# Retention in half chunks: 64x64 products in place of 64x128 and 128x64 ones, state summed in PSUM, GEMM products from chunk 5 on

## The chip, the core and the metric

The kernel runs on one core of a Trainium2 chip. The metric is the device time of one execution, in microseconds. The kernel before took 580.88 us (median of 3 runs, 578.93 to 582.52).

## What is computed

Retention over 2 batches x 8 heads x 768 positions with head dimension 64, then two MLPs over the 1536 resulting rows, all in float32:

```python
for t in range(S):
    state = gamma[None, :, None, None] * state + np.einsum('bhd,bhe->bhde', k[:, :, t], v[:, :, t])
    y[:, :, t] = scale * np.einsum('bhd,bhde->bhe', q[:, :, t], state)
...
h = x @ w_in                                  # 1536x512 @ 512x2048
sp = np.where(h > 20.0, h, np.log1p(np.exp(np.minimum(h, 20.0))))
x = (h * np.tanh(sp)) @ w_out                 # 2048x512
h = x @ w2_in
out = (h * np.cos(h)) @ w2_out
```

The weights arrive as float64 bits; the kernel splits them, and the activations, into a high and a low part, so that each product of a GEMM is three fp32r products (high x high, high x low, low x high).

## The kernel before

**Retention.** The 1536 positions are 12 chunks of 128: chunks 0 to 5 are the first sequence, 6 to 11 the second. q, k, v of a chunk are one load of 1 MiB (`att_load`, in two halves for chunks 0 to 4: first q and k, then v and k in the other layout). For each chunk TensorE does four groups of 8 fp32 products; an fp32 product stands in the trace as two matmul records, so a group is "x16":

- scores (`att_scores`, L330): k times q of the chunk, 64 rows and 128 columns of the array, 128 columns moved; VectorE multiplies the result with a mask of decays (`att_mask`, L335)
- inter (`att_inter`, L376): the state of the chunks before times the scaled q, 64x64 of the array, 128 columns moved; not in chunks 0 and 6
- update (`att_update`, L346): k times the scaled v, 128x64 of the array, 64 columns moved; VectorE adds it to the decayed state (`att_state`, L353, L355), and GpSimd decays the state for the next chunk (`att_scaled`)
- out (`att_out`, L387): v times the masked scores, 128x64 of the array, 128 columns moved; then ScalarE and VectorE split the result into the high and the low part of x (L401, L404)

GpSimd makes the scaled q (`att_qd`) and the scaled v (`att_vd`; ScalarE makes that of chunks 1 to 4).

**GEMMs.** Four chunks make one block of 512 rows of x. A GEMM product of the first kind (`gemm1`, L427) takes 128x128 weights and 512 moved columns. A weight item is named by (which, group, half): ("i", 0, 0) is the first half of the first group of w_in, in two pieces n = 0, 1 of 512 KiB. Pieces of the first w_in are loaded "crossed" (three transfers of 64 or 128 partitions with runs of 1 KiB, L210 and L213), except the `EARLY` one, which is loaded whole (L207) and crossed by the split instead (`w_rows`). The first 96 GEMM products are dealt between the chunks, from chunk 3 on (`deal`); the second GEMM (`gemm2`, L450) starts when retention is over and its PSUM is free (`close`).

**Order.** A planner (`Plan`) takes TensorE's order as the code writes it, and sets the order of the other queues, SP's loads among them, by a list schedule over costs in the code.

Of the kernel before, what the change touches and what calls it, by code (L numbers as in the profile page):

```python
# [20 lines left out]
C = 128  # L21
# [11 lines left out]
VD_ACT = (1, 5)  # L33
EARLY = (("i", 0, 0), 0)
QD_DVE = ()
# [8 lines left out]
TERMS = ((0, 0), (0, 1), (1, 0))  # L44


def shape_constants():
    gamma = (1.0 - 2.0 ** (-5.0 - np.arange(H, dtype=np.float32))).astype(np.float64)
    i = np.arange(C, dtype=np.float64)
    half = np.arange(128) // D  # L50

    doublings = 2.0 ** np.arange(7)
    heads = [2 * a + e for e in range(2) for a in range(NPAIR)]
    first = gamma[heads][None, :] ** -i[:, None] / math.sqrt(D)
    grow = np.broadcast_to(gamma[heads][None, None, :] ** doublings[None, :, None], (128, 7, 8))
    upper = (i[None, :] >= i[:, None]).astype(np.float64)
    of = np.stack([gamma[2 * a + half] for a in range(NPAIR)], axis=1)
    first_q = of / math.sqrt(D)
    grow_q = of[:, None, :] ** doublings[None, :, None]
    decv = gamma[None, :] ** (C - 1.0 - i[:, None])  # L60
    parts = [decv, of**C, first, grow, first_q, grow_q, upper]
    packed = np.concatenate([p.reshape(128, -1) for p in parts], axis=1)
    return np.ascontiguousarray(packed.astype(np.float32))


class Plan:
# [47 lines left out]
    def order(self):  # L114
# [20 lines left out]
        free = {o["engine"]: 1.4 if o["engine"] == "SP" else 0.0 for o in ops}  # L135
        pool = shared = (0.0, 0.0)
        self.start, self.end, order = {}, {}, []
        while ready:
# [32 lines left out]
def retention_two_mlps(ctx: ExitStack, tc: tile.TileContext, qkv, w1i, w1o, w2i, w2o, consts, out):  # L171
# [25 lines left out]
    def w_load(it, ns):  # L197
# [74 lines left out]
    def w_low_part(it, ns, single):  # L272
        eng = nc.vector if single else nc.gpsimd
        for to, of in w_rows(it, ns):
# [12 lines left out]
    scaled = {}  # L287
    update = {}
# [20 lines left out]
    def att_vd(g, part):  # L309
# [3 lines left out]
        if not VD_ACT[0] <= g < VD_ACT[1]:  # L313
            nc.gpsimd.tensor_mul(out=vd[g], in0=v, in1=decv.unsqueeze(2).to_broadcast([128, H, D]))
            return
        for h in range(H // 2 * part, H // 2 * (part + 1)):
            nc.scalar.activation(out=vd[g][:, h, :], in_=v[:, h, :], func=AF.Copy, scale=decv[:, h : h + 1])

    def att_qd(g, eng):
        qd[g] = att_p.tile([128, NPAIR, C], F32, tag="qd", name="qd")  # L320
        eng.tensor_mul(out=qd[g], in0=qk_of(g)[:, :, 0, :], in1=decq)


    def att_scores(g):
        qk = qk_of(g)
        ss = ps_p.tile([128, 2, NPAIR, C], F32, tag="s", name="ps_s")
        for a in range(NPAIR):
            for e in range(2):
                h = slice(D * e, D * e + D)
                nc.tensor.matmul(ss[:, e, a, :], qk[h, a, 1, :], qk[h, a, 0, :], start=True, stop=True)  # L330
        pm[g] = ss

    def att_mask(g):
        p = att_p.tile([128, 2, NPAIR, C], F32, tag="p", name="p")
        nc.vector.tensor_mul(  # L335
            out=p.rearrange("p e a b -> p (e a b)"), in0=pm[g].rearrange("p e a b -> p (e a b)"), in1=mask
        )
        pm[g] = p

    def att_update(g):  # L340
        kn = att[g][:, 1536:2048].rearrange("p (a b) -> p a b", a=NPAIR)
        ps = ps_p.tile([128, NPAIR, D], F32, tag="u", name="ps_u", bufs=2)
        for a in range(NPAIR):
            for e in range(2):
                h = slice(D * e, D * e + D)
                nc.tensor.matmul(ps[h, a, :], kn[:, a, h], vd[g][:, 2 * a + e, :], start=True, stop=True)  # L346
        update[g] = ps


    def att_state(g):  # L350
        state[g] = att_p.tile([128, NPAIR, D], F32, tag="st", name="st")
        if g % NCH == 0:
            nc.vector.tensor_copy(out=state[g], in_=update[g])  # L353
        else:
            nc.vector.tensor_add(out=state[g], in0=update[g], in1=scaled[g])  # L355

    def att_scaled(g):
        scaled[g + 1] = att_p.tile([128, NPAIR, D], F32, tag="sc", name="scaled")
        nc.gpsimd.tensor_mul(out=scaled[g + 1], in0=state[g], in1=carry)

    def y_tag(g):
        return "h0" if g in (0, 2) else "y"

    def att_y(g):
        if g not in y_t:
            pool, tag = (h_p, "h0") if y_tag(g) == "h0" else (ps_p, "y")
            ps = pool.tile([128, 2, BLK], F32, tag=tag, name="ps_y")
            y_t[g] = ps[:, :, 0 : BLK // 2].rearrange("p r (s c) -> p r s c", c=C)
        return y_t[g]

    def att_inter(g):
        ps = att_y(g)
        for a in range(NPAIR):
            for e in range(2):
                h = slice(D * e, D * e + D)
                nc.tensor.matmul(  # L376
                    ps[y_rows(a, e), a % 2, a // 2, :], state[g - 1][h, a, :], qd[g][h, a, :],
                    start=(a < 2), stop=False, skip_group_check=True,
                )

    def att_out(g):
        c = g % NCH
        v = att[g][:, 1024:1536].rearrange("p (h d) -> p h d", h=H)
        ps = att_y(g)
        for a in range(NPAIR):
            for e in range(2):
                nc.tensor.matmul(  # L387
                    ps[y_rows(a, e), a % 2, a // 2, :], v[:, 2 * a + e, :], pm[g][:, e, a, :],
                    start=(c == 0), stop=True, skip_group_check=True,
                )  # L390

# [141 lines left out]
    def weight(it, between=lambda: None):  # L533
        raw, mag, w = ("raw", it), ("mag", it), ("w", it)
        first, single = it[:2] == ("i", 0), it[:2] in (("i", 0), ("o", 0), ("i", 1))
        slow = [1.5 if it[0] == "i" and it[1] < NG and (it, n) != EARLY else 1.0 for n in range(2)]
        if single:
            loads = [op("SP", 1.25 * slow[0], w_load, it, (0,), new=(raw, 2))]
            between()
            loads.append(op("SP", 1.25 * slow[1], w_load, it, (1,), uses=[raw]))  # L540
        else:
            loads = [op("SP", 2.5 * slow[0], w_load, it, (0, 1), new=(raw, 2))]
        for load, ns in zip(loads, [slice(0, 1), slice(1, 2)] if single else [slice(0, 2)]):
# [11 lines left out]
            early, sign = (it, ns.start) == EARLY, last  # L555
# [5 lines left out]
            def high_op(needs):  # L561
                return op("ACT", 1.08 if early else 1.08 * c, w_high_part, it, ns, needs=needs, uses=[mag, w])
# [6 lines left out]
            for n in range(ns.start, ns.stop):  # L569
                at["wh", it, n] = high  # L570
            on_dve = single
            last = op(
                *(("DVE", 1.3 if early else 0.72) if on_dve else ("POOL", 2.45 * c)), w_low_part, it, ns, on_dve,
                needs=[high, low], uses=[w, raw if single else mag],
            )
# [17 lines left out]
    def chunk_pre(g):  # L593
        c = g % NCH
        key = chunk(g)
        on_act = VD_ACT[0] <= g < VD_ACT[1]
        if c + 1 < NCH:
            at["vd", g] = [
                op(
                    *(("ACT", 0.98) if on_act else ("POOL", 1.15)), att_vd, g, part, needs=at["v", g] + at["dec"],  # L600
                    new=None if part else (("vd", g), 2), uses=[key, ("vd", g)],
                )
                for part in range(2 if on_act else 1)
            ]
        if c > 0:
            name, cost, eng = ("DVE", 0.72, nc.vector) if g in QD_DVE else ("POOL", 1.3, nc.gpsimd)
            at["qd", g] = op(
                name, cost, att_qd, g, eng, needs=at["qk", g] + at["decq"], new=(("qd", g), 2), uses=[key]
            )

    def chunk_scores(g):
        s = ("s", g)
        at["s", g] = op("PE", 1.1, att_scores, g, needs=at["qk", g], new=(s, 1, "s"), uses=[chunk(g)])
        at["p", g] = op("DVE", 1.25, att_mask, g, needs=[at["s", g]] + at["mask"], new=(("p", g), 2), uses=[s])

    def chunk_update(g):
        c = g % NCH
        if c + 1 == NCH:
            return
        u = ("u", g)  # L620
        at["u", g] = op(
            "PE", 0.62, att_update, g, needs=at["vd", g] + at["k", g], new=(u, 2), uses=[chunk(g), ("vd", g)]
        )
# [297 lines left out]
```

## Time and profile before

| | |
|---|---|
| median of 3 runs | 580.88 us (578.93 to 582.52) |
| profiled execution, its own time | 582.62 us |
| its span, first to last instruction | 580.8 us |
| end of the last TensorE group | 577.6 us from the span's start |
| TensorE busy | 570.0 us (98%) |
| DMA busy share, 20 to 40 us | 1.0 (326 and 317 GB/s) |

All times in the views are microseconds from the start of the span. "Idle before" an instruction is the time in which its engine had nothing to run, with the engine or transfer whose end released it. PEclk is the granted clock of TensorE as a share of 2.4 GHz.

### The profile page before, as it was taken

To read this page: it belongs to the slowest core of one execution; us is meant where nothing else is said; L and a number is where in the kernel's file an instruction comes from. 1 tells how busy PE (TensorE), PEld (TensorE's weight loads), DVE (VectorE), ACT (ScalarE), POOL (GpSimd) and SP (SyncE) were. 2 spreads that over 40 slices of the span, in tenths; PEclk is the share of its full clock that TensorE was granted. 3 is DMA by queue.
4 is the path that set the end of the run, shared out by engine and by line. 5 is a ranking of instruction groups with operands and counts; after the bars stand their busy time and mean duration, and the time that the engine had idled before them with its cause. 6 is when DMAs were issued, how large, how long until landed. Compare 5 with 4: busy or idle time off the path is not lost.

```text
span 580.8 us, 7248 instructions
## 1 busy us (share of the span) xinstructions
PE 570.0 (98%) x3054; PEld 469.2 (81%) x3054; DVE 385.1 (66%) x410; ACT 225.5 (39%) x255; POOL 96.2 (17%) x63
## 2 busy tenths in 40 slices
PE   8789999999999999999999999999999999999997
PEld 6567888888888888888888888888888888888886
DVE  5678889744185524655377995988588994865462
ACT  3633343334023123123235564575254353354240
POOL 5355100212011111102011102023010403000000
PEclk9989999999999999999999999999999999999999
DMA  8996044353004220312003031224003020000103
GB/s 294 310 290 247 30 145 143 104 159 103 0 9 137 74 72 1 144 73 72 1 19 127 1 106 40 73 72 146 0 1 122 24 73 1 0 1 0 73 36 109
DMA packets 19952, 49.87 MB, mean 86 GB/s; under 512 B 2000, under 2 KB 10064, under 8 KB 19024
## 3 DMA queue, kind: packets, MB, share of 16 engines
q1 hardware_dynamic: 19920, 49.41, 25.2%
q8 instruction: 24, 0.39, 0.3%
q14 instruction: 8, 0.07, 0.0%
HBM read 46.26 MB, written 3.15 MB: 85 GB/s over the span
## 4 chain that ended last, share of the span: by engine, by line
PE 93%; DMA 5%; SPq 1%; ACT 0%; DVE 0%; issue 0%; DVEq 0%; ACTq 0%
PE ps_o L450 45%; PE ps_h L427 45%; DMA qkv<-qkv_dram 4%; DMA raw<-w1i_dram 2%; PE ps_s L330 1%; PE ps_y L387 1%; PE ps_y L376 1%; SPq L304 0%; PE ps_u L346 0%; ACT L454 0%; DVE p L335 0%; ACT mag L218 0%; ACT x L401 0%; DVE acc L515 0%; SPq L740 0%
## 5 line engine op out<-in xcount | busy, mean ns | idle before, releaser
L427 PE MATMUL ps_h<-x,wi 128*128 128x512 f32 x1152 | 268.2, 391 | 0.9 <-DVE wi L275 0.4
L427 PEld LDWEIGHTS ps_h<-x,wi 128*128 128x128 f32 x1152 | 215.7, 188 | 47.6 <-DVE wi L275 1.2
L450 PE MATMUL ps_o<-wo,g 128*128 128x512 f32 (+1 forms) x588 | 132.5, 385 | 0.0
L450 PE MATMUL ps_o<-g,wo 128*128 128x512 f32 x576 | 132.3, 389 | 0.0
L450 PEld LDWEIGHTS ps_o<-wo,g 128*128 128x128 f32 x588 | 108.9, 188 | 22.0
L450 PEld LDWEIGHTS ps_o<-g,wo 128*128 128x128 f32 x576 | 108.1, 188 | 22.4
L492 DVE TENSOR_TENSOR g<-mish,g 128x1024 fp32r<-128x1024 f32 x24 | 33.7, 1404 | 56.6 <-ACT g L488 55.6
L275 POOL TENSOR_TENSOR wo<-mag,wo 128x1024 fp32r<-128x1024 f32 x14 | 35.4, 2526 | 202.4 <-ACT wo L261 202.4
L508 DVE TENSOR_TENSOR acc<-ps_o,acc 128x1024 f32<-128x1024 f32 x35 | 42.7, 1221 | 34.6 <-PE ps_o L450 34.4
L275 POOL TENSOR_TENSOR wi<-mag,wi 128x1024 fp32r<-128x1024 f32 x12 | 30.2, 2520 | 194.1 <-ACT wi L261 194.1
L458 ACT ACTIVATE mish<-ps_h 128x1024 f32<-128x1024 f32 x24 | 24.7, 1029 | 92.1 <-PE ps_h L427 92.1
L472 DVE SCALAR_TENSOR_TENSOR turns<-whole,turns 128x1024 f32<-128x1024 f32 x24 | 29.3, 1222 | 44.8 <-ACT whole L468 44.8
L464 ACT ACTIVATE turns<-ps_h,quarter 128x1024 f32<-128x1024 f32 x24 | 26.7, 1113 | 65.4 <-PE ps_h L427 65.1
L241 DVE SCALAR_TENSOR_TENSOR mag<-raw,mag 128x1024 uint32<-128x1024 uint32 (+1 forms) x38 | 40.7, 1072 | 1.1
L481 ACT ACTIVATE turns<-turns 128x1024 f32<-128x1024 f32 x24 | 25.5, 1062 | 34.8 <-DVE turns L478 34.6
L492 DVE TENSOR_TENSOR g<-turns,g 128x1024 fp32r<-128x1024 f32 x24 | 33.2, 1383 | 8.0 <-ACT g L488 8.0
L484 DVE TENSOR_TENSOR turns<-turns,ps_h 128x1024 f32<-128x1024 f32 x24 | 29.2, 1215 | 10.1 <-ACT turns L481 6.8
L267 DVE SCALAR_TENSOR_TENSOR mag<-raw,mag 128x1024 uint32<-128x1024 uint32 x26 | 33.7, 1300 | 0.4
L488 ACT CAST g<-turns 128x1024 fp32r<-128x1024 f32 x24 | 25.1, 1045 | 17.0 <-DVE turns L484 16.9
L261 ACT CAST wi<-mag 128x1024 fp32r<-128x1024 f32 (+3 forms) x22 | 18.1, 821 | 30.9 <-DVE mag L267 25.8
L225 DVE TENSOR_SCALAR mag<-raw 128x1024 uint32<-128x1024 uint32 (+1 forms) x34 | 22.3, 669 | 9.7 <-POOL wo L275 5.6
L261 ACT CAST wo<-mag 128x1024 fp32r<-128x1024 f32 (+1 forms) x18 | 17.2, 955 | 27.9 <-PE ps_o L450 20.6
(50 smaller groups left out, 344.0 us busy)
## 6 DMA issues: line engine op xcount, KB each, us to landing
raw<-w1o_dram SPq DMA_DIRECT2D x16, 512.0 KB, 4.2
raw<-w2i_dram SPq DMA_DIRECT2D x16, 512.0 KB, 4.2
raw<-w2o_dram SPq DMA_DIRECT2D x16, 512.0 KB, 3.8
qkv<-qkv_dram SPq DMA_DIRECT2D x7, 1024.0 KB, 6.4
qkv<-qkv_dram SPq DMA_DIRECT2D x10, 512.0 KB, 9.0
raw<-w1i_dram SPq DMA_DIRECT2D x15, 256.0 KB, 4.0
raw<-w1i_dram SPq DMA_DIRECT2D x30, 128.0 KB, 4.0
out_dram<-acc SPq DMA_DIRECT2D x11, 256.0 KB, 2.3
```

The source lines that it names most:

```text
L241: nc.vector.scalar_tensor_tensor(out=a, in0=high, scalar=0xC0000000, in1=a, op0=ALU.bitwise_and, op1=ALU.bitwise_or)
L261: nc.scalar.copy(out=to(w_t[it][:, :, 0]), in_=of(mag_t[it]).bitcast(F32))
L267: nc.vector.scalar_tensor_tensor(out=w_all_of(it, single)[:, ns], in0=raw_t[it][:, ns, :, 0], scalar=29, in1=mag_t[it][:, ns], op0=ALU.log ...
L275: eng.tensor_sub(out=to(w_t[it][:, :, 1]), in0=of(w_all_of(it, single)).bitcast(F32), in1=to(w_t[it][:, :, 0]).bitcast(F32),)
L427: nc.tensor.matmul(h_t[k][:, f % 2, :], w[:, f % 2, a, kk * 128 : (kk + 1) * 128], x[:, b, kk, :], start=(a + b + kk == 0), stop=(a == 1 a ...
L450: nc.tensor.matmul(ps, lhs, rhs, start=(n == 0), stop=(n == 3 * GF - 1))
L464: nc.scalar.activation(out=t_t[k], in_=h_t[k], func=AF.Identity, scale=INV_2PI, bias=quarter)
L472: nc.vector.scalar_tensor_tensor(out=t, in0=n_t[k], scalar=MAGIC, in1=t, op0=ALU.subtract, op1=ALU.subtract)
L481: nc.scalar.activation(out=t_t[k], in_=t_t[k], func=AF.Sin, scale=-TWO_PI)
L484: nc.vector.tensor_mul(out=t_t[k], in0=t_t[k], in1=h_t[k])
L492: nc.vector.tensor_sub(out=g[:, :, 1, :], in0=t_t[k], in1=g[:, :, 0, :].bitcast(F32))
L508: nc.vector.tensor_add(out=acc, in0=o_t[m * NG + G, j, p], in1=acc)
```

## The change

A chunk is worked on as two halves of 64 positions, and every retention product is a 64x64 quarter of the array with 64 columns moved. The state of a sequence is summed in one PSUM tile over its six chunks: v is scaled by the decay up to the end of the sequence, q by the inverse of it, so that nothing is decayed in between. ScalarE copies the sum to SBUF after each half (`att_state`). TensorE's groups of a chunk are now: first (8 products), update of half 0 (8), the scores of the next chunk (16), second (8 inter with 8 update of half 1, in turn), third (16). GpSimd makes all scaled v but that of chunk 0; VectorE makes five tables of q decays (`att_decq`). Both pieces of ("i", 0, 0) are loaded whole, the mask is half as wide, and the first GEMM product comes after chunk 5.

```diff
-VD_ACT = (1, 5)
-EARLY = (("i", 0, 0), 0)
+HC = C // 2
+VD_ACT = ()
+VD_DVE = (0,)
+EARLY = ("i", 0, 0)
+DECQ_DVE = (1, 2, 3, 4, 5)
+Y_TAGS = ("h0", "y") * 3 + ("y",) * 6
+MISH = 4
+DEAL = {
+    5: [(0, 0, (0, 1, 2, 3)), (0, 1, (0, 1, 2, 3))],
+    6: [(0, 2, (0, 1, 2, 3))],
+    7: [(0, 3, (0, 1, 2, 3))],
...
+    11: [(1, 3, (0, 1, 2, 3))],
+}
...
+    QUARTERS = ((0, 0), (1, 1), (0, 1), (1, 0))
...
     def att_scores(g):
         qk = qk_of(g)
-        ss = ps_p.tile([128, 2, NPAIR, C], F32, tag="s", name="ps_s")
+        ss = ps_p.tile([128, 2, BLK], F32, tag="s", name="ps_s")
+        pm[g] = ss[:, :, 0 : BLK // 2].rearrange("p e (a b) -> p e a b", a=NPAIR)
         for a in range(NPAIR):
-            for e in range(2):
-                h = slice(D * e, D * e + D)
-                nc.tensor.matmul(ss[:, e, a, :], qk[h, a, 1, :], qk[h, a, 0, :], start=True, stop=True)
+            for e, h in QUARTERS:
+                product(pm[g][rows(h), e, a, :], qk[rows(e), a, 1, rows(h)], qk[rows(e), a, 0, rows(h)], True)
...
+    def update(g, h):
...
+        def one(a, e):
+            product(
+                t[rows(e), a, :], kn[rows(h), a, rows(e)], vd[g][rows(h), 2 * a + e, :], first_in(t, e)
+            )
...
+    def att_first(g):
+        side_by_side(outputs(g, 0, 1), outputs(g, 1, 0))
+
+    def att_second(g):
+        side_by_side(inter(g, 0, 1) + inter(g, 0, 0), update(g, 1) if g % NCH + 1 < NCH else [])
+
+    def att_third(g):
+        side_by_side(outputs(g, 0, 0), inter(g, 1, 1) + inter(g, 1, 0) + outputs(g, 1, 1))
...
+    def att_state(g, h):
+        state[g, h] = att_p.tile([128, NPAIR, D], F32, tag="st", name="st", bufs=4)
+        nc.scalar.copy(out=state[g, h], in_=total[g // NCH])
...
-    chunk_loads(3, (0, 1024))
-    weight(("i", 0, 0), lambda: chunk_loads(3, (1024, 2048)))
+    weight(("i", 0, 0), lambda: chunk_loads(3, (0, 1024, 2048)))
...
+    for n in range(NCHK):
         if n + 1 < NCHK:
             chunk_pre(n + 1)
-        chunk_inter(n)
-        chunk_update(n)
-        chunk_out(n)
+        chunk_first(n)
         if n + 1 < NCHK:
             chunk_scores(n + 1)
+        chunk_second(n)
+        if n == MISH:
+            at["table"] = op("ACT", 1.6, mish_table, needs=[at["act", ("i", 0, 1), 1]])
         products(n)
```

TensorE around the first GEMM products; before, they follow the scores of chunk 4, the first row here:

```order
L330 MATMUL ps_s<-qkv 128x128 x8
L427 MATMUL ps_h<-x,wi 128x512 x6
L376 MATMUL ps_y<-qd,st 64x128 x8
L346 MATMUL ps_u<-vd,qkv 64x64 x8
L387 MATMUL ps_y<-p,qkv 64x128 x8
L330 MATMUL ps_s<-qkv 128x128 x8
L427 MATMUL ps_h<-x,wi 128x512 x6
```

With the change, from the end of chunk 4 (its last inter products and outputs; in the row x12 its last 4 outputs and first of chunk 5; then update of chunk 5, the scores of chunk 6 and inter of chunk 5):

```order
L368 MATMUL ps_y<-qd,st 64x64 x5
L368 MATMUL ps_y<-p,qkv 64x64 x12
L368 MATMUL ps_u<-vd,qkv 64x64 x8
L368 MATMUL ps_s<-qkv 64x64 x16
L368 MATMUL ps_y<-qd,st 64x64 x8
```

and behind the outputs of chunk 5:

```order
L368 MATMUL ps_y<-p,qkv 64x64 x4
L493 MATMUL ps_h<-x,wi 128x512 x24
L368 MATMUL ps_y<-p,qkv 64x64 x8
L368 MATMUL ps_u<-vd,qkv 64x64 x8
L368 MATMUL ps_s<-qkv 64x64 x16
```

The scores of chunk 6 now stand ahead of every GEMM product; before, 12 GEMM products stood ahead of them.

VectorE at the end of retention, before (L404 is the low part of x of chunk 11, L275 the last step on a piece of ("o", 0, ·), L225 the first step on a piece: in the first row on the last one of ("o", 0, 1), in the last row on the first one of ("i", 1, 0), which waits for its load):

```order
L225 TENSOR_SCALAR mag<-raw 128x512
L404 TENSOR_TENSOR x<-ps_y,x 128x2x2x128
L275 TENSOR_TENSOR wo<-raw,wo 128x512
L231 TENSOR_SCALAR mag<-mag 128x512
L235 TENSOR_SCALAR mag<-mag 128x512
L241 SCALAR_TENSOR_TENSOR mag<-raw,mag 128x512
L267 SCALAR_TENSOR_TENSOR raw<-raw,mag 128x512
L492 TENSOR_TENSOR g<-mish,g 128x2x512
L275 TENSOR_TENSOR wo<-raw,wo 128x512
L225 TENSOR_SCALAR mag<-raw 128x512
```

With the change (L470 is the low part of x, of chunk 10 and then of chunk 11; L242 is the first step on a piece, here on ("i", 1, 0)):

```order
L292 TENSOR_TENSOR wo<-raw,wo 128x512
L470 TENSOR_TENSOR x<-ps_y,x 128x2x2x128
L258 SCALAR_TENSOR_TENSOR mag<-raw,mag 128x512
L284 SCALAR_TENSOR_TENSOR raw<-raw,mag 128x512
L292 TENSOR_TENSOR wo<-raw,wo 128x512
L242 TENSOR_SCALAR mag<-raw 128x512
L470 TENSOR_TENSOR x<-ps_y,x 128x2x2x128
```

The low part of x of chunk 11 now stands behind a step that waits for the load of ("i", 1, 0); before it stood ahead of it.

## Rows read from the trace of the kernel before

**Rows 1.** The page: span, and busy time by engine.

```profile
span 580.8 us, 7248 instructions
PE 570.0 (98%) x3054; PEld 469.2 (81%) x3054; DVE 385.1 (66%) x410; ACT 225.5 (39%) x255; POOL 96.2 (17%) x63
```

**Rows 2.** TensorE's longest wait to 80 us: line, releaser, total us, times, longest.

```profile
PE ps_y L387 <- DVE p L335: 2.3, 1, 2.3
```

**Rows 3.** Windows: stretch, length, busy of PE, PEld, DVE, ACT, POOL, PEclk, DMA share, GB/s.

```profile
20.00:30.00 10.00, 8.06 (x122) 5.79 (x124) 8.30 (x16) 7.29 (x23) 2.96 (x4) 1.00 1.06 326
30.00:40.00 10.00, 7.66 (x96) 5.85 (x96) 7.00 (x10) 3.60 (x6) 5.14 (x4) 1.00 1.01 317
...
36.80:40.23 3.43, 1.09 (x25) 0.95 (x26) 2.34 (x3) 1.05 (x3) 2.26 (x2) 1.00 0.99 406
40.23:43.64 3.41, 3.41 (x29) 2.86 (x26) 2.89 (x5) 1.21 (x2) 2.89 (x3) 0.50 0.55 180
```

**Rows 4.** The chain that ended last, in time: start, us, what.

```profile
39.77 1.57 PE ps_y L387 x16
...
48.27 2.97 PE ps_h L427 x12
...
74.02 13.83 PE ps_h L427 x60
...
109.60 10.88 PE ps_h L427 x48
...
555.68 21.92 PE ps_o L450 x108
```

**Rows 5.** TensorE by time: chunk 3, then chunk 8; some windows cut a group.

```profile
20.70 0.67 PE L376 MATMUL ps_y<-qd,st 64*64 64x128 f32 x16 [2.24 <-DVE st L355]
...
51.16 0.67 PE L376 MATMUL ps_y<-qd,st 64*64 64x128 f32 x16
51.54 0.29 PE L376 MATMUL ps_y<-qd,st 64*64 64x128 f32 x4
51.76 0.45 PE L346 MATMUL ps_u<-vd,qkv 128*64 128x64 f32 x8
51.76 0.69 PE L346 MATMUL ps_u<-vd,qkv 128*64 128x64 f32 x16
...
53.25 1.16 PE L330 MATMUL ps_s<-qkv 64*128 64x128 f32 x16
54.34 0.50 PE L427 MATMUL ps_h<-x,wi 128*128 128x512 f32 x1
```

**Rows 6.** Line L376 from 50 to 54 us: ns min/median/max of one record.

```profile
L376 PE MATMUL ps_y<-qd,st x16: 269/269/321, 51.2 to 51.6; 64*64 64x128 f32 x16
```

**Rows 7.** GpSimd and ScalarE instructions that waited for loads: chunks 2, 3, 4 and 6.

```profile
11.97 1.27 POOL L321 TENSOR_TENSOR qd<-qkv,cst 128x512 f32<-128x512 f32 x1 [1.52 <-DMA qkv<-qkv_dram]
14.65 1.27 POOL L321 TENSOR_TENSOR qd<-qkv,cst 128x512 f32<-128x512 f32 x1 [0.83 <-DMA qkv<-qkv_dram]
33.05 1.57 POOL L314 TENSOR_TENSOR vd<-qkv,cst 128x512 f32<-128x512 f32 x1 [1.74 <-DMA qkv<-qkv_dram]
...
25.06 2.02 ACT L317 ACTIVATE vd<-qkv,cst 128x64 f32<-128x64 f32 x8 [0.55 <-DMA qkv<-qkv_dram]
```

**Rows 8.** Groups by line from 43.64 to 72 us: busy, mean ns; idle, releaser.

```profile
L492 DVE TENSOR_TENSOR g<-mish,g 128x1024 fp32r<-128x1024 f32 x3 | 3.6, 1216 | 0.0
L401 ACT CAST x<-ps_y 128x512 fp32r<-128x512 f32 x4 | 2.3, 587 | 4.6 <-PE ps_y L387 4.6
L458 ACT ACTIVATE mish<-ps_h 128x1024 f32<-128x1024 f32 x3 | 3.1, 1027 | 7.8 <-PE ps_h L427 7.8
L346 PE MATMUL ps_u<-vd,qkv 128*64 128x64 f32 x64 | 2.7, 228 | 0.0
```

**Rows 9.** SP's first issue for ("i", 1, 0), and VectorE's first step on it.

```profile
76.01 0.56 SPq L210 DMA_DIRECT2D raw<-w1i_dram  x1
...
81.05 0.43 DVE L225 TENSOR_SCALAR mag<-raw 128x512 uint32<-128x512 uint32 x1
```

More of the change, by code (lines that the diff above doesn't have):

```diff
@@ L286, in retention_two_mlps @@
     state = {}
-    scaled = {}
-    update = {}
+    total = {}
+    decq = {}
+    begun = set()
     pm = {}
@@ L338, in att_mask @@
+        nc.vector.tensor_mul(out=p, in0=pm[g], in1=m)
         pm[g] = p
-    def att_update(g):
[L341 to L355, printed above, removed]
@@ new lines, in y_at, with inter, one, outputs @@
+    def y_at(g, a, e, h):
+        n = e ^ (a % 2)
+        return att_y(g)[rows(n), a % 2, a // 2, h, :], first_in(y_t[g], n, a % 2)
+    def inter(g, e, h):
+        s = state[g, 0] if h else state[g - 1, 1] if g % NCH else None
+        if s is None:
+            return []
+        def one(a):
+            y, first = y_at(g, a, e, h)
+            product(y, s[rows(e), a, :], qd[g][rows(e), a, h, :], first)
+        return [(lambda a=a: one(a)) for a in range(NPAIR)]
+    def outputs(g, e, h):
+        v = att[g][:, 1024:1536].rearrange("p (h d) -> p h d", h=H)
+        def one(a):
+            y, first = y_at(g, a, e, h)
+            product(y, v[rows(h), 2 * a + e, :], pm[g][rows(h), e, a, :], first)
+        return [(lambda a=a: one(a)) for a in range(NPAIR)]
@@ L595, in chunk_pre @@
         key = chunk(g)
[L596 to L608, printed above, removed]
-            )
+        on_act = g in VD_ACT
@@ L671, in tile_in @@
         if m == 0:
-            last = op("ACT", 1.06, mish, k, needs=[last, table], new=(t, 3), uses=[h])
+            last = op("ACT", 1.06, mish, k, needs=[last, at["table"]], new=(t, 3), uses=[h])
         else:
@@ L746, in grow @@
         eng.tensor_copy(out=t[:, :, 0:1], in_=few(at_first, n).unsqueeze(2))
-        for k in range(7):
+        for k in range(6):
             w = 2**k
@@ L791, in retention_two_mlps, with products @@
-    later = {1: [("i", 0, 1)], 3: [("o", 0, 0)], 5: [("o", 0, 1)], 7: [("i", 1, 0)], 9: [("i", 1, 1)]}
+    last = op("DVE", 1.2, att_mask_grow, needs=[load], uses=["few"])
+    at["mask"] = [op("DVE", 0.65, att_mask_upper, needs=[last], uses=["few"])]
+    at["decq0"] = at["dec"] = [op("POOL", 2.4, att_decq_grow, needs=[load], uses=["few"])]
+    def products(n):
+        for i, f, *rest in DEAL.get(n, ()):
+            tile_in(*steps[i], f, *rest)
     chunk_pre(0)
     chunk_scores(0)
-    op("PE", 1.1, zeros, 10, "u")
```

318 lines of the change are left out of this document (165 added, 153 removed).

## The prediction

> **What bounds the kernel now.** First the page: TensorE is busy for 570.0 of 580.8 us [rows 1]. The reader is to see that no stage after retention has anything to give: from 74.02 us to the last TensorE group, which ends at 555.68 + 21.92 = 577.6 us, the chain of waits is TensorE alone, at 10.88 us per 48 products (0.227 us each) [rows 4]. So the end is the moment from which TensorE never waits again, plus the work that it then still has. Second the waits and the windows before that moment: the last long wait, 2.3 us, is that of the outputs of chunk 6 for the masked scores; it ends at 39.77 us [rows 2, 4]. In that time the DMA share is 1.0 [rows 3]: loads pace retention, and VectorE (8.3 of 10 us) and ScalarE (7.3) are well filled too. Behind the wait the granted clock is 0.50 for 3.41 us, TensorE's lower level of 1.2 GHz, after a stretch in which TensorE was busy for 1.09 of 3.43 us [rows 3]; that costs half of 3.41, 1.7 us. Third TensorE by time in a chunk without waits: how long each group of products takes, and how many run at once [rows 5].
>
> My forecast is made against the profiled execution, 582.62 us with TensorE's end at 577.6; the median shown is 1.7 us less, and I move the difference that I find onto the median.
>
> **The new products.** In inter, on 64x64 quarters, the last four records lie within 0.29 us, and one lasts 0.269 [rows 5, 6]: they started within 0.02 us and ran side by side. So 16 records are four rounds. In update, with 64 columns moved and two records at once, records 9 to 16, four rounds, take 0.69 - 0.45 = 0.24 us: 0.06 a round. No row has four quarters with 64 columns moved. The price is at least that of the update round, 0.06, since as many columns move, and at most the share of a round in inter, 0.60 / 4 = 0.15, which moves twice as many. I take 0.06, the row with the same 64 columns.
>
> A full chunk now has 64 products, 128 records. First, scores, second fill four quarters (4 + 8 + 8 rounds); update of half 0 uses two (8); in third the upper rows have 12 products on two quarters (12). That is 40 rounds, 2.4 us. Before, a chunk took 51.16 to 54.34, 3.18 us, with three changes of shape inside [rows 5]; the new groups have one shape, and only the change to the GEMM products stays. From scores to GEMM the rows give 1.09 for 8 rounds; I put 0.15 on a change. So 2.55 against 3.18: 0.6 us less per chunk.
>
> The rule that speaks against this stands in the Trainium skill, "TensorE: Matmul & The Clock Gate", section "Back-to-back issue gap": matmuls never start closer than about 25 ns, however few columns move. By it a round of four would take an estimated 0.1 us in place of 0.06, and the time would be an estimated 589.8, between the third and the fourth rival. The trace of inter disagrees: its four records started within the 0.02 us above.
>
> **The loads up to chunk 6.** The order rows show what is moved most: the scores of chunk 6 stand ahead of all GEMM products. Until chunk 6 has landed, TensorE has nothing but chunks 0 to 5, some 2.5 us each, against 2.7 for a load of two plain halves and more where a weight piece lies between, and it waits. So the moment from which it is never idle long is the landing of chunk 6. Before, it landed at 33.05 [rows 7]. The bytes ahead of it stay the same; one crossed piece becomes a plain one. Between the first half of chunk 3 (14.65) and the second of chunk 4 (25.06) lie four plain halves and that crossed one, 10.41 us; a plain half takes (14.65 - 11.97) / 2 = 1.34 [rows 7]. That leaves 5.05 us for the crossed one and what it holds up. Plain, it saves 3.7 us at most, and nothing at least, if another load holds the queue up as long. I take 2.0, the middle, since a second crossed piece still stands ahead: chunk 6 at 31.0, bounds 29.4 and 33.05. SP issues it once chunk 3's buffer is free, a chunk's work after chunk 4 landed, with chunk 5 and a crossed piece still in the queue to cover that.
>
> **What is left for TensorE at 31.0.** 256 rounds (20 of chunk 5, 48 of scores, 28 of chunk 6, 4 x 32, 32) at 0.06: 15.4. The 84 GEMM products dealt to chunks 5 to 10 at 0.227: 19.0. Six entries into them at 2.97 - 12 x 0.227 = 0.25 [rows 4]: 1.5. Seven changes out of retention at 0.15: 1.0. From the 12 products of chunk 11 on as before, 577.6 - 74.02 = 503.6.
>
> **The state copy** is a new wait. Update's last record ends 0.23 us after its start [rows 8]; ScalarE's copy of 128x256 is worked out from 587 ns for 512 columns and 1027 for 1024 [rows 8], 0.37; with two hand-overs of some 0.1 that is 0.8, against 8 rounds of scores, 0.48, as cover: 0.3 per chunk for chunks 6 to 10, and 0.8 for chunk 11, which has no scores behind it: 2.3. At least 0; at most one mish (1.03) more each time. The second copy has third and the GEMM products as cover. Behind the copies on ScalarE wait the split of x and mish, which have a chunk's 5 us.
>
> **The clock.** TensorE now waits some 3 us each for chunks 5 and 6, like the stretch that came before the 0.50. I expect it again, as one or two such stretches after 31.0: 1.7 to 3.4, I take 2.5; at least 0.
>
> **At no cost.** VectorE loses half of each mask product and all state adds, and gains five tables and one scaled v. GpSimd gains six scaled v, at most 1.57 each [rows 7], and loses eight decays; both have 5 us per chunk once GEMM products run, and if that cover goes, the masked scores are late first. The split of ("i", 0, 0) is needed only at about 32 us. At the end of retention VectorE's low part of x of chunk 11 stands behind the first step on ("i", 1, 0). From its issue (76.01) to that step (81.05) were at most 5.0 us [rows 9]. SP now issues it when the last step on ("o", 0, 0) frees the buffer. By the sum below TensorE begins the 12 products of chunk 11 at 72.7, so those of chunk 9 end at 72.7 - 5.8 - 2.9 = 64.0 (chunks 10 and 11). Then follow mish 1.03, a state copy 0.37, a cast of 1.05, VectorE's low part of g 1.2, the last step 0.7 [rows 8] and 0.4 of hand-overs: issue at 68.8, low part of x at 68.8 + 5.0 + 0.4 + 0.7 = 74.9. TensorE wants it at 72.7 + 2.7 = 75.4. At most 2 us if one is off.
>
> **Sum.** 31.0 + 15.4 + 19.0 + 1.5 + 1.0 + 503.6 + 2.3 + 2.5 = 576.3, against 577.6: 1.3 us less. On the median: **579.6 us**. The cheaper products are real, some 0.6 us in each of twelve chunks; they go into waits for loads that the GEMM products of chunks 3 and 4 used to fill.
>
> **Rivals.**
> 1. *Faster.* The crossed piece was what held the loads up, and chunk 6 lands at 29.4; the clock stays at 2.4 GHz, or its low stretch lies in the waits for loads; state copies cost half. -1.6 - 2.5 - 1.2: 574.3. For it: the loads before 14.65 came every 1.34 us [rows 7]; the wait of 2.24 us that ended at 20.70 was followed by no low clock [rows 3, 5]. Against: one crossed piece stays ahead.
> 2. *Slower, through ScalarE.* The state copy stands in line behind a mish or a cast of about 1.03 us: up to 1.0 more per chunk for six chunks, 585.6. It decides if ScalarE begins such a step less than 0.3 us before update ends. For it: mish starts when a GEMM pair ends, which is just before first and update. Against: only every second chunk ends a pair. With a late low part of x (2 us) it ends above 587.
> 3. *Slower, since the quarters don't fill.* If only two records run at once, the 20 rounds of first, scores and second double: half of 256 rounds more, 7.7 us: 587.3. Then the change would not do what it says. Four side by side in inter speak against it.
> 4. *Slower, since a record's start costs and not its columns.* Then a round keeps inter's 0.15: 256 x 0.09 = 23.0 more, 602.6. Against it: update's rounds, with 64 columns, take 0.06. The page on the clock gate named above is the milder form of it.
>
> **Chances.** Forecast 0.70; faster rival 0.15, about its own time; ScalarE 0.07, half of it below the bound; quarters 0.06, starts 0.02. What a measurement of this kernel can tell from no change is 1%, so the bounds are 575.1 and 586.7: faster 0.15, within 0.73, slower 0.12. The range takes in the faster rival and the unknown costs (landing 29.4 to 33.05, clock 0 to 3.4, copies 0 to 8): 574 to 586.
>
> **What would show it.** Right: records of the new products four at a time, 40 rounds in 2.4 us; waits of the scores of chunks 5 and 6 for loads, about 3 us each; the scores of chunk 6 at 31.0; 0.3 us before second in chunks 6 to 10; a stretch at 0.50 after 31. Wrong: a round above 0.08, chunk 6 before 29 or after 33, a long wait before the first product of block 2 for x, or TensorE waiting for masked scores beside GEMM products.

## The result, and the profile after

The changed kernel takes 588.62 us (median of 4 runs, 587.77 to 590.07), the kernel before 580.97 beside it (578.93 to 582.52): ratio 1.0136, 95% interval 1.0097 to 1.0175. The forecast was 579.6 in a range of 574 to 586. The profiled execution took 590.07 us, so it lies 1.5 us above its median; its TensorE ends at 585.0 us of the span, 7.4 later than before.

The page of the changed kernel answers to [rows 1]. The third line is the queue that brings instructions: packets, MB, share.

```profile
span 588.3 us, 8772 instructions
PE 572.1 (97%) x3822; PEld 476.0 (81%) x3822; DVE 391.2 (66%) x407; ACT 224.9 (38%) x247; POOL 96.4 (16%) x61
q8 instruction: 30, 0.49, 0.3%
```

TensorE runs 768 more records and as many more weight loads. The 0.49 MB are 64 bytes for each of its 3822 + 3822 instructions: q8 carries TensorE's program, in 30 packets of 16 KB, 256 instructions each. In the kernel before it brings 24 packets for 3054 + 3054.

TensorE's waits of the changed kernel [rows 2]:

```profile
PE ps_s L368 <- issue: 4.7, 3, 2.1
PE ps_s L368 <- DMA qkv<-qkv_dram: 4.5, 3, 3.0
PE ps_y L368 <- DVE p L387: 1.1, 1, 1.1
```

The first row is new in kind: "issue" is time in which TensorE waited for nothing that the profile shows. I call it a standstill.

Windows of the changed kernel, cut where the granted clock changes [rows 3]:

```profile
8.00:14.91 6.91, 4.44 (x160) 3.83 (x159) 6.91 (x9) 1.71 (x4) 5.46 (x4) 1.00 1.02 392
14.91:28.56 13.65, 10.76 (x332) 10.57 (x333) 8.23 (x11) 5.12 (x12) 5.51 (x5) 0.50 0.49 185
28.56:31.98 3.42, 1.15 (x50) 1.01 (x45) 2.36 (x5) 1.12 (x3) 0.00 (x0) 1.00 1.04 331
31.98:45.63 13.65, 12.10 (x218) 10.78 (x219) 9.31 (x14) 5.92 (x12) 6.75 (x6) 0.50 0.73 255
45.63:56.00 10.37, 10.23 (x204) 8.37 (x202) 7.36 (x11) 4.30 (x8) 3.01 (x2) 1.00 0.54 207
```

The granted clock is 0.50 (1.2 GHz) twice for 13.65 us, where before it was so once for 3.41. And from 14.91 to 28.56 the DMA share is only 0.49: the loads no longer pace that stretch.

TensorE by time in the changed kernel, chunk 2, then 5, 6, 7 and 11 [rows 5]. L368 is the helper that issues every product, so the tiles tell the groups apart.

```profile
13.13 0.40 PE L368 MATMUL ps_s<-qkv 64*64 64x64 f32 x8
15.68 0.60 PE L368 MATMUL ps_s<-qkv 64*64 64x64 f32 x13 [2.15 <-issue]
...
32.69 0.48 PE L368 MATMUL ps_s<-qkv 64*64 64x64 f32 x6 [2.98 <-DMA qkv<-qkv_dram]
...
37.75 0.48 PE L368 MATMUL ps_s<-qkv 64*64 64x64 f32 x5 [0.36 <-DMA qkv<-qkv_dram]
38.71 1.01 PE L368 MATMUL ps_s<-qkv 64*64 64x64 f32 x26 [0.48 <-issue]
...
41.62 0.79 PE L493 MATMUL ps_h<-x,wi 128*128 128x512 f32 x1
...
54.75 0.46 PE L368 MATMUL ps_y<-p,qkv 64*64 64x64 f32 x16
55.41 0.28 PE L368 MATMUL ps_s<-qkv 64*64 64x64 f32 x2
...
56.25 0.24 PE L368 MATMUL ps_y<-qd,st 64*64 64x64 f32 x1
...
56.36 0.22 PE L368 MATMUL ps_u<-vd,qkv 64*64 64x64 f32 x1
56.37 0.22 PE L368 MATMUL ps_y<-qd,st 64*64 64x64 f32 x1
56.38 0.22 PE L368 MATMUL ps_u<-vd,qkv 64*64 64x64 f32 x1
56.38 0.22 PE L368 MATMUL ps_y<-qd,st 64*64 64x64 f32 x1
...
57.57 3.01 PE L493 MATMUL ps_h<-x,wi 128*128 128x512 f32 x12
...
80.08 0.70 PE L368 MATMUL ps_y<-qd,st 64*64 64x64 f32 x19 [0.69 <-ACT st L447]
81.32 3.24 PE L493 MATMUL ps_h<-x,wi 128*128 128x512 f32 x13
```

Three things are to be seen. The scores of chunk 2 stop in the middle of their group for 2.15 us, with operands long there: the first 8 records of the group ran. The scores of chunk 6 start at 37.75, where the forecast had 31.0. And once products of the GEMM run, a chunk is as cheap as forecast: chunk 7 takes 54.75 to 57.57, 2.82 us, with four records starting within 0.02 us.

SP's issues of the loads of chunks 5, 6 and 7:

```profile
25.43 0.33 SPq L322 DMA_DIRECT2D qkv<-qkv_dram  x1
...
29.16 0.35 SPq L322 DMA_DIRECT2D qkv<-qkv_dram  x1
...
36.33 5.77 SPq L322 DMA_DIRECT2D qkv<-qkv_dram  x2
```

GpSimd's wait for chunk 6 ends 4.7 us later than in [rows 7]:

```profile
37.78 1.32 POOL L334 TENSOR_TENSOR vd<-qkv,cst 128x512 f32<-128x512 f32 x1 [2.79 <-DMA qkv<-qkv_dram]
```

The chain of the changed kernel has the same pieces [rows 4]:

```profile
20.18 2.12 issue
...
29.16 8.46 DMA qkv<-qkv_dram
...
41.69 7.56 PE ps_h L493 x24
```

24 products take 7.56 us here, of which the part up to 45.63 runs at the low clock; at 0.227 each they take 5.45.

What happens at the standstills shows in the instruction queue. The DMA view of the changed kernel from 13.2 to 14.3, and from 19.8 to 21.0 us:

```profile
q8 instruction: 1, 0.02, 5.5%
...
q8 instruction: 1, 0.02, 5.8%
```

One 16 KB packet lies in each; their records begin at 13.24 and 19.83 and last 1.0 and 1.1 us. TensorE stops at 13.53 and 20.18, and goes on at 15.68 and 22.31, each time 2.4 to 2.5 us after the packet began. The windows from packet to work:

```profile
13.24:15.68 2.44, 0.29 (x13) 0.15 (x5) 2.15 (x2) 0.37 (x1) 2.44 (x2) 0.84 1.00 405
19.83:22.31 2.48, 0.36 (x11) 0.17 (x5) 1.91 (x3) 0.37 (x1) 1.05 (x1) 0.50 0.09 30
```

The DMA engines are full in the first (share 1.00) and nearly idle in the second (0.09), and the time is the same. So here loads did not stretch the time behind the packet's start; what they can have done is put off that start.

### The profile page after: what moved, and what is told of

Its sections match the earlier page's. It is cut to its first block, busy times and chain, and to the rows that moved or that the text cites. A ratio compares the mean times of both kernels' runs of the same rounds, so it can differ in the third digit from the quotient of the medians.

```text
span 588.3 us, 8772 instructions
## 1 busy us (share of the span) xinstructions
PE 572.1 (97%) x3822; PEld 476.0 (81%) x3822; DVE 391.2 (66%) x407; ACT 224.9 (38%) x247; POOL 96.4 (16%) x61
## 4 chain that ended last, share of the span: by engine, by line
PE 91%; DVE 4%; DMA 2%; issue 1%; ACT 1%; SPq 0%; ACTq 0%
PE ps_o L516 44%; PE ps_h L493 43%; DMA qkv<-qkv_dram 2%; PE ps_y L368 2%; PE ps_s L368 1%; PE ps_u L368 1%; DVE p L387 1%; DVE mag L258 1%; DVE decq L349 0%; DVE x L470 0%; DVE mag L248 0%; DVE mag L252 0%; DVE raw L284 0%; DVE wo L292 0%; DVE g L558 0%
## 5 line engine op out<-in xcount | busy, mean ns | idle before, releaser
L558 DVE TENSOR_TENSOR g<-mish,g 128x1024 fp32r<-128x1024 f32 x24 | 35.0, 1459 | 53.0 <-ACT g L554 53.0
L538 DVE SCALAR_TENSOR_TENSOR turns<-whole,turns 128x1024 f32<-128x1024 f32 x24 | 29.4, 1223 | 40.5 <-ACT whole L534 40.4
L558 DVE TENSOR_TENSOR g<-turns,g 128x1024 fp32r<-128x1024 f32 x24 | 35.9, 1496 | 7.2 <-ACT g L554 7.2
L547 ACT ACTIVATE turns<-turns 128x1024 f32<-128x1024 f32 x24 | 25.5, 1062 | 37.6 <-DVE turns L544 37.5
L550 DVE TENSOR_TENSOR turns<-turns,ps_h 128x1024 f32<-128x1024 f32 x24 | 29.2, 1216 | 12.6 <-ACT turns L547 9.2
L242 DVE TENSOR_SCALAR mag<-raw 128x1024 uint32<-128x1024 uint32 (+1 forms) x34 | 23.4, 701 | 17.7 <-DMA raw<-w1i_dram 9.3
L554 ACT CAST g<-turns 128x1024 fp32r<-128x1024 f32 x24 | 25.1, 1046 | 19.5 <-DVE turns L550 19.5
L544 DVE TENSOR_SCALAR turns<-turns 128x1024 f32<-128x1024 f32 x24 | 29.1, 1214 | 0.8
```

Of the source, the lines that this page charges most:

```text
L538: nc.vector.scalar_tensor_tensor(out=t, in0=n_t[k], scalar=MAGIC, in1=t, op0=ALU.subtract, op1=ALU.subtract)
L544: nc.vector.tensor_scalar(out=t, in0=t, scalar1=-0.5, scalar2=0.5, op0=ALU.max, op1=ALU.min)
L547: nc.scalar.activation(out=t_t[k], in_=t_t[k], func=AF.Sin, scale=-TWO_PI)
L550: nc.vector.tensor_mul(out=t_t[k], in0=t_t[k], in1=h_t[k])
L558: nc.vector.tensor_sub(out=g[:, :, 1, :], in0=t_t[k], in1=g[:, :, 0, :].bitcast(F32))
```

## Experiments

The theories at the start were A (the low clock), B (loads that wait for buffers) and C (the form of the products, with twice the instructions); after the first four runs C became S, the supply of instructions. Ratios are to the kernel before, with 95% intervals. "First" and "25th" are the starts of those GEMM products, "end" is TensorE's last, "still" is the sum of the "issue" waits, "low" the time at 1.2 GHz before 60 us; all in us, of the profiled execution.

| run | median | ratio | first | 25th | end | still | low |
|---|---|---|---|---|---|---|---|
| before | 580.97 | | 24.6 | 48.2 | 577.6 | 0 | 3.4 |
| after | 588.62 | 1.0136 (1.0097 to 1.0175) | 41.6 | 51.8 | 585.0 | 4.7 | 27.3 |
| deal3 | 587.45 | 1.0102 (1.0052 to 1.0153) | 29.1 | 56.0 | 585.5 | 4.3 | 23.9 |
| old_from5 | 581.64 | 1.0004 (0.9975 to 1.0033) | 32.9 | 41.2 | 576.7 | 0 | 0 |
| warm_fill | 588.70 | 1.0119 (1.0073 to 1.0165) | 42.5 | 50.8 | 585.4 | 6.6 | 6.8 |
| more_bufs | 585.68 | 1.0078 (1.0056 to 1.0100) | 37.6 | 46.3 | 580.6 | 7.0 | 20.5 |
| old_short | 586.48 | 1.0090 (1.0075 to 1.0105) | 31.4 | 51.5 | 580.8 | 3.4 | 3.4 |
| shallow | 586.74 | 1.0108 (1.0074 to 1.0142) | 39.5 | 49.0 | 582.0 | 3.6 | 17.1 |
| old5_bufs | 581.90 | 1.0009 (0.9990 to 1.0027) | 34.0 | 42.2 | 575.6 | 0 | 3.4 |
| shallow_bufs | 588.18 | 1.0117 (1.0091 to 1.0144) | 40.1 | 48.8 | 583.0 | 4.3 | 10.2 |
| mixed | 582.77 | 1.0030 (1.0017 to 1.0043) | 31.1 | 43.9 | 577.7 | 0 | 3.4 |
| old5_bufs_y | 581.42 | 1.0017 (0.9997 to 1.0037) | 32.7 | 41.0 | 577.3 | 0 | 3.4 |

**Form or place of the products: deal3 and old_from5.**

```diff
 # deal3: the changed kernel, dealt as before
-    5: [(0, 0, (0, 1, 2, 3)), (0, 1, (0, 1, 2, 3))],
+    3: [(0, 0, (0, 1))], 4: [(0, 0, (2, 3))], 5: [(0, 1, (0, 1))], 6: [(0, 1, (2, 3))],
 # old_from5: the kernel before, dealt as in the change
-        3: [(0, 0, first)], 4: [(0, 0, second)], 5: [(0, 1, first)], 6: [(0, 1, second)],
+        5: [(0, 0, whole), (0, 1, whole)],
```

> The 64x64 products stay, the GEMM products are dealt as in the kernel before, from chunk 3 on. Theory A (the two stretches of 13.65 us at 1.2 GHz come from TensorE having only retention work with waits until 41.7 us): with GEMM products from about 27 us the second low stretch is gone, the first may stay; end of TensorE 576 to 579, median 578 to 582. Theory B (chunk 5 and 6 land late because their loads wait for a buffer of the chunk three before): the landings stay near 32.6 and 37.6, but the waits are filled with GEMM products; some 580 to 583. Theory C (the form of the new products, with twice the instructions, is at fault): 586 or more, with waits of the class 'issue' as before.

> The kernel before with its own retention, only the GEMM products dealt as in the changed one, from chunk 5 on. Theory A and B (the place of the products, not their form): TensorE waits for chunks 5 and 6 without other work; the 24 products of chunks 3 and 4 (5.4 us) fall behind the wait that ends at 39.77, so 3 to 7 us more than before, 584 to 588, and a long low stretch if retention alone does not lift the clock. Theory C (the form): no more than 2 us over before, at most 583.

The move alone costs nothing measurable (1.0004), and taking it back gains nothing measurable (1.0102; the interval overlaps that of after). So it is the form of the new retention, or its number of products, and my expectation from the place was wrong in both runs. With the old products TensorE waits for loads too (1.9 us in all), and the granted clock is 1.0 throughout; with the new ones the standstills at the first two fetches stay. Theory C holds, and the idea that a late first product costs time by itself falls.

**The clock: warm_fill.**

```diff
         chunk_first(n)
+        if n < 6:
+            op("PE", 0.1, zeros, 6 if n < 4 else 24, "w")
         if n + 1 < NCHK:
             chunk_scores(n + 1)
```

> The changed kernel with products of zeros (128x128 bf16, 256 columns) ahead of the next chunk's scores: 6 each in chunks 0 to 3, 24 each in chunks 4 and 5. Nothing else is moved. Theory A: TensorE is busy in the waits, the granted clock is 1.0 from the first chunk on or the low stretches are much shorter; half of the 12.1 us of work at the low clock between 31.98 and 45.63 comes back, 6 us, less at most 1 us for the zeros: 582 to 584. Theory B alone: the clock may rise but chunk 6 still lands at 37.6; 586 to 589.

Windows of warm_fill, the same stretch as in the table of after, and its one low stretch:

```profile
31.98:45.63 13.65, 11.92 (x258) 10.14 (x256) 8.15 (x14) 5.75 (x11) 5.96 (x6) 1.00 0.82 248
...
20.06:26.89 6.83, 5.61 (x130) 4.84 (x132) 1.46 (x3) 1.25 (x4) 0.84 (x1) 0.50 0.03 9
```

The second low stretch is gone, and the time is the same. The 24 products take 5.7 us instead of 7.6, but three standstills, now 3.6, 1.6 and 1.4 us long, and the zeros themselves eat that up. The first product is no earlier (42.5 for 41.6), so the second low stretch is a cost in its place and not the reason that retention is late. The first low stretch is only shortened, to 6.8 us, so this run does not settle what it costs.

**The loads: more_bufs.**

```diff
-        if not att:
+        if g < 4 and g not in att:
             t = x_p.tile([128, 2, KD, BLK], F32R, tag="x", name="qkv")
...
-        return ("qkv", max(g, 1))
+        return ("qkv", 1 if g < 2 else 3 if g < 4 else g)
```

> The changed kernel with chunks 2 and 3 loaded into a second x buffer that is free until chunk 4 writes x, so that the loads of chunks 4, 5 and 6 wait for no buffer. Theory B: chunk 5 lands at 26 to 28 and chunk 6 at 29 to 31 in place of 32.6 and 37.6; TensorE has work from then on, end 4 to 7 us earlier, 582 to 585 even if the low clock stays. Theory A alone (the low clock sets the pace of retention, the loads only seem late): 586 to 588, with chunk 6 in SBUF long before TensorE gets to it.

Waits and a window of more_bufs:

```profile
PE ps_s L368 <- issue: 7.0, 3, 2.5
...
PE ps_s L368 <- DMA qkv<-qkv_dram: 0.4, 1, 0.4
```

```profile
14.13:34.61 20.48, 15.17 (x460) 14.79 (x461) 12.06 (x17) 6.45 (x15) 7.92 (x8) 0.50 0.75 258
```

Chunk 6 is there at 26.4 in place of 37.6, and the wait for loads falls from 4.5 us to 0.4. That is worth 2.9 us on the median, between the two expectations: TensorE now reaches the scores of chunk 6 at about 35, nine us after the load. What holds it are three standstills of 2.1 to 2.5 us, and the low clock that begins in the first. So the late loads are a part of it, and themselves made by the late TensorE.

**The number of instructions alone: old_short.**

```diff
+    def short(n):
+        ps = ps_p.tile([128, 256], F32, tag="u", name="ps_w", bufs=2)
+        for i in range(n):
+            e = h = i % 2
+            left = zero[D * e : D * e + D, 0:D]
+            nc.tensor.matmul(ps[D * h : D * h + D, 0:16], left, left[:, 0:16], start=True, stop=True, skip_group_check=True)
...
         chunk_out(n)
+        op("PE", 1.0, short, 64)
```

> The kernel before, with 64 short products of zeros (64x64 bf16, 16 columns, about 1 us in all) behind the outputs of each of the chunks 0 to 3. They change no result; they double the instructions that TensorE reads in the stretch up to 25 us and hardly its work. Theory S (TensorE's instructions arrive in pieces of 16 KB, about 256 matmul and weight-load instructions, and while the loads fill the DMA engines a piece comes only every 6 to 7 us): TensorE stands still for about 2 us at each of the fetches near 13 and 20 us, without a wait that the profile shows, as in the changed kernel; it loses 3 to 5 us in chunks 0 to 3, 583 to 587. Theory F (the form of the 64x64 fp32 products or their waits, not the number of instructions): no standstill at the fetches; the short products fall into the waits for loads, 581 to 583.

TensorE by time in old_short, in the outputs of chunk 2, and its windows between its first three fetches:

```profile
20.38 0.82 PE L387 MATMUL ps_y<-p,qkv 128*64 128x128 f32 x10
24.05 0.65 PE L387 MATMUL ps_y<-p,qkv 128*64 128x128 f32 x6 [2.86 <-issue]
```

```profile
14.10:21.37 7.27, 6.58 (x172) 5.40 (x170) 2.84 (x5) 4.54 (x17) 2.57 (x4) 1.00 1.06 299
21.37:25.77 4.40, 1.72 (x74) 1.54 (x78) 4.37 (x6) 1.91 (x6) 2.02 (x2) 1.00 1.04 241
```

The old products now stand still too, in the middle of a group of the old shape, for 2.86 us; the packet lies in that time, from 21.37 on, and work goes on 2.7 us after it began. At the first fetch (14.10) there was no long one. The kernel before ran 213 instructions in the stretch between its first two fetches, this one 342. The window of before:

```profile
14.49:21.68 7.19, 4.95 (x108) 4.07 (x105) 4.09 (x8) 4.05 (x15) 2.57 (x3) 1.00 1.06 308
```

So more instructions bring the standstill to products of the old shape too. The end is 3.3 us later than before in the profiled execution, and the median 5.4. The short products are not as cheap as I expected: TensorE is busy with them for 5.0 us, partly in what were waits, so what the standstill costs by itself isn't told apart here.

**The queue ahead of a fetch: shallow.**

```diff
+        if (g, lo) in BEHIND:
+            of, at_col = BEHIND[g, lo]
+            nc.scalar.copy(out=att[g][:, lo : lo + 1], in_=att[of][:, at_col : at_col + 1])
         eng.dma_start(out=att[g][:, lo:hi], in_=qkv[g, :, lo:hi])
```

> The changed kernel, with the loads of chunks 2 to 4 each issued only when a load two to three halves earlier has landed (ScalarE writes one column of the target from it first), so that 3 to 4 us of loads stand in the queue at a time in place of some 10. Theory Q (the fetch of instructions stands in line behind the loads already issued): the fetches near 13 and 20 us come 2 us or more earlier by the count of instructions run, the two standstills of 2.1 us shrink below 1 us, and the low clock that begins in the first of them is gone or shorter; 581 to 585. Theory R (a fetch begins only when the instructions have run out, or the engines are full however short the queue): standstills stay at about 2 us; 587 to 590, since the loads themselves come no earlier.

Windows of shallow up to its first fetch and between the next two:

```profile
0.00:10.59 10.59, 9.23 (x178) 7.14 (x178) 6.47 (x16) 2.78 (x7) 5.21 (x15) 1.00 0.76 259
10.59:15.78 5.19, 3.41 (x144) 2.99 (x144) 4.65 (x6) 1.53 (x5) 3.51 (x3) 1.00 0.88 301
15.78:21.23 5.45, 4.28 (x132) 4.03 (x134) 2.75 (x5) 2.32 (x7) 2.75 (x3) 0.73 0.89 291
```

TensorE's standstills in shallow:

```profile
PE ps_s L372 <- issue: 3.6, 5, 1.4
```

The first two of these windows in after:

```profile
0.00:13.24 13.24, 10.01 (x218) 8.00 (x220) 8.25 (x19) 2.91 (x5) 7.10 (x16) 1.00 0.84 293
13.24:19.83 6.59, 4.44 (x139) 4.30 (x131) 4.20 (x4) 1.89 (x4) 3.85 (x4) 0.63 0.93 377
```

With fewer loads in the queue the first fetch starts after 356 instructions in place of 438, and the next 5.2 us later in place of 6.6. The standstills at the first three fetches are 0.3, 0.2 and 1.0 us, and the first low stretch is 3.4 us long. So the loads ahead of it are part of what makes a fetch late. The gain is small and not clear of the noise, 1.9 us on the medians with intervals that overlap: chunk 5 still waits for a buffer (issued at 20.9), the standstills at the next two fetches are 1.4 and 0.7 us, and TensorE now waits for the loads that were held back (0.8 us before the second standstill).

**Both: shallow_bufs.** The two diffs above in one kernel.

> The changed kernel with both edits: loads of chunks 2 to 4 issued only when a load two to three halves earlier has landed, and chunks 2 and 3 in a second x buffer, so that loads of 4, 5 and 6 wait for no buffer. If late fetches and late buffers are the causes of the late first GEMM product (41.6 us, against 32.9 with the old retention and the same deal), they add up: standstills below 1 us, chunk 6 landed before 31, first GEMM product at 33 to 36, TensorE's end at 576 to 579, 578 to 582. If the supply of instructions is the limit however short the queue (some 256 per 5 us, two thirds of what a chunk every 3.2 us wants), TensorE stands still for shorter times but more of them: first product still at 37 or later, end at 580 to 582, 583 to 586.

The pessimistic half came, and worse: standstills are short up to 30 us, but at 34.1 one of 3.2 us follows, at a fetch that begins at 34.57, and the queued loads of chunks 5 and 6 land late, at 29.5 and 33.3. So the two causes did not add up: the first product, at 40.1, is no earlier than with either edit alone. Between 10.8 and 34.6 us the packets came every 5.4 to 6.9 us, a block of 256 instructions and so a chunk each. That this is the pace that the fetches set is not shown: until 34.1 the standstills are only 1.2 us in all, and TensorE waits 5.9 us for held-back loads, masked scores, scaled v and VectorE.

**Old retention with the early loads: old5_bufs and old5_bufs_y.** The diff of more_bufs on old_from5, and in the second also:

```diff
-        return "h0" if g in (0, 2) else "y"
+        return "h0" if g in (0, 2, 4) else "y"
```

> The old retention with the GEMM products from chunk 5 on and with chunks 2 and 3 loaded into a second x buffer, so that the loads of chunks 4, 5 and 6 wait for no buffer. Theory S: with 64 products a chunk there is no standstill at fetches, so what the loads gain reaches the end: chunk 6 lands near 30 in place of 31.7, the waits at 27 and 42 to 49 us (4.8 us in all with those behind the weights) shrink, 577 to 581. If the loads of the weights are now what comes late (the first w_in pieces stand behind chunks 5 and 6): 581 to 584, with the waits of the first GEMM products longer.

> The old retention with products from chunk 5 on and the second x buffer, and the outputs of chunk 4 in the PSUM of h0 (free until the first GEMM product) in place of the y bank that chunk 3 still holds. In the run without that, TensorE waited 3.2 us for VectorE's low part of x on that bank, the longest 1.8 us before chunk 4 or 5. If TensorE is what is late there: first GEMM product 1 to 2 us earlier than 34.0, TensorE's end at 573.5 to 575, 579 to 580.5, a gain of 0.2 to 0.4% over the kernel before. If VectorE is the bound of that stretch (its split of x and of weights): the wait turns into one for masked scores or weights, 580 to 582.

Both give no measurable difference to before. The expected gains of 1 to 2 us turned into another wait each time. In old5_bufs_y the first product is 1.3 us earlier, and TensorE then waits for the split of the weights:

```profile
PE ps_h L427 <- DVE wi L275: 1.8, 1, 1.8
```

**Whole chunks first, half chunks later: mixed.** On the diff of more_bufs. `chunk_whole` issues inter, update and out, 8 products each of the old shapes, and the mask is 128 wide until chunk 5. Up to chunk 2 the scores of the next chunk stand ahead of the chunk, and six GEMM products of chunk 10 move into chunk 11.

```diff
+WHOLE = 6
...
+        if n < WHOLE:
+            chunk_whole(n)
+        else:
             chunk_first(n)
             chunk_scores(n + 1)
+            if n + 1 == NCHK:
+                tile_in(*steps[1], 2, (2, 3))
             chunk_second(n)
```

> Sequence 1 (chunks 0 to 5) in whole chunks with 64 products of the old shapes each, or fewer, the state still summed in PSUM; sequence 2 (chunks 6 to 11), which runs between GEMM products, in half chunks of 64x64 products; second x buffer for the loads; 6 products of the GEMM between the two halves of chunk 11, so that the state copy is covered. If the instructions' supply is the cause: no standstill at a fetch, first GEMM product at 32 to 35 as with the old retention, and the 3.5 us that the half chunks saved between products 24 and 72 are kept, end at 571 to 574, 575 to 578. If the half chunks' gain is lost anyway (state copies, low clock): 579 to 582.

Waits of mixed:

```profile
PE ps_h L534 <- DVE wi L294: 2.3, 2, 1.4
PE ps_y L370 <- DVE p L396: 2.0, 2, 1.0
PE ps_s L385 <- DVE p L396: 1.1, 1, 1.1
```

No standstill, and the first product at 31.1, as theory S has it or a little earlier: the state in PSUM and the 64x64 products behind chunk 5 bring no standstill. But the time is above both expectations and does not beat the kernel before (1.0030). VectorE, which makes five tables, whole masks and the split of the weights, is late now; and the half chunks themselves gain little. From the 25th to the 85th product mixed takes 29.5 us and old5_bufs 29.8: 0.3 to 0.4 us less in each of chunks 7 to 9, 0.1 more in chunk 10, and 0.7 more in chunk 11, which in the old form has no update and no state to copy. No version tried here is faster than the kernel before.

## Why the prediction was wrong

**What bounds the kernel** was right: from the 85th product (81.32) to the end are 503.6 us, as forecast.

**The new products** were right: second and third, 20 rounds, take 56.25 to 57.57 with the change to the GEMM, 1.32 us, or 20 x 0.06 and the 0.15. On the rule of the Trainium skill, "TensorE: Matmul & The Clock Gate", section "Back-to-back issue gap": the trace disagrees here as in the prediction, with four starts within 0.02 us, so that floor does not bind four quarters of the array side by side. **The state copy** was right: from scores to second 0.84 us in chunk 7 (0.84 to 0.93 in chunks 6 to 10) against 0.48 of rounds, 0.36 for 0.3; in chunk 11 0.69 for 0.8. **At no cost** held: no wait for the low part of x of chunk 11 shows between 81.32 and the next step.

**"The loads up to chunk 6"** is the step that failed: "chunk 6 at 31.0, bounds 29.4 and 33.05". The loads did gain: the last half of chunk 4 lands at 22.6 in place of 25.0. But I had the loads set the pace of TensorE, "some 2.5 us each", and chunk 5 "still in the queue". TensorE took 6.4 to 6.6 us a chunk, with a standstill of 2.1 us in each and the low clock from the first one on (scores of chunk 2 from 13.0, of chunk 3 from 19.5, of chunk 4 from 26.1), so the load of chunk 5 waited for chunk 2's buffer until 25.4, that of chunk 6 for chunk 3's until 29.2, and chunk 6 landed at 37.6. The scores of chunk 6 started 6.75 us after the forecast. That TensorE could be short of instructions was in none of my rivals.

**What was left behind that moment** was 41.7 us by forecast and 43.57 by trace (37.75 to 81.32). Of the 1.9, a standstill is 0.5. **The clock** is 1.2: from 37.75 to 45.63 are 7.4 us of work at half clock, so 3.7 lost for the 2.5 that I took. The sum had no low stretch ahead of chunk 6's landing, and the 2.24 us wait of before was followed by none. Here one came, from 14.91 on, inside a standstill of 2.15 us; its cost is in the 6.75 and isn't told apart from that of the standstills. 6.75 + 1.9 is the whole miss of 8.7 us in TensorE's end, 585.0 for 576.3.

**What I could have read.** The order showed twice the records per chunk, and I priced only their time in the array. By the window of before above, 213 instructions run in 7.19 us between two fetches, 30 per us, without a standstill. A new chunk has 256, and I had it done in 2.5 us: 102 per us, over three times as many, while the DMA share is 1.0. No row of before had the limit, but that distance was reason enough for a rival. The Trainium skill, "Runtime: NRT & Kernel Launch", section "Instruction fetch mechanics", says that an engine's instructions come in blocks of 16 KiB, 256 of them, that the next one is fetched while the current one runs, and that crossing into it is mostly hidden. The blocks agree with the 30 packets of 0.49 MB. The crossing was not always hidden here: it cost 2.15 and 2.12 us in after, 2.86 with the old products in old_short, and nothing at the fetch of after that began at 23.43.

## What to carry to other kernels

Count TensorE's instructions per microsecond before cutting products into smaller ones: in this kernel, while loads kept the DMA share at 0.88 or more, 30 to 38 per us ran between two fetches without a standstill (before, mixed) and 39 to 55 with one (more_bufs, shallow), where the changed kernel wanted 102. With the loads at a DMA share of 0.45 some 70 per us ran without one (after, 23.43 to 29.27 us). Cheaper products gained nothing here in a stretch that ends on loads, and buffers tied the two together: a TensorE that falls behind frees them late, and the loads then come late as well. Undo the parts of a change one by one; the part that looked dangerous, moving the GEMM products, cost nothing.

## What the runs showed of the hardware

- TensorE stood still for up to 3.6 us (warm_fill) with all operands there, at the fetch of its next 16 KB of instructions. In after the packets began 0.3 us before TensorE stopped, and work went on 2.4 to 2.5 us after they began; in the other runs with standstills that last time was 2.2 to 2.8 us.
- In after that time was the same with and without loads: 2.44 us at a DMA share of 1.00, 2.48 at 0.09.
- The start of a fetch did go with the loads. In the ten runs that issue the first loads without a delay the first fetch begins at 12.4 to 14.5 us, whether TensorE has run 228 instructions by then (mixed) or 441 (more_bufs); with fewer loads queued it begins at 10.6 (shallow), after 356. A fetch that stands in line behind the loads would look like this; the runs don't show the line itself.
- The first stretch at 1.2 GHz lasted 13.65 us in after, with TensorE busy for 10.76 of them, and 20.48 in more_bufs, busy for 15.17. Both stretches began inside the first standstill, and both ended before any GEMM product. Waits of 1.2 to 1.6 us in old_from5 were followed by no low stretch. What the clock answers to was not settled.
